# The last block of a fused recurrence and MLP kernel: two single-quadrant products in banks of their own, and the fallback path as a loop

## The chip, the cores and the metric

One core of a Trainium2 chip. The time is device microseconds of one execution, 2330.94 us for the kernel before (median of three runs, 2330.39 to 2331.64). Besides it this document uses a second measure: the **tail**, read from a trace. Its zero, the **anchor**, is the start of a product of one column, called `most`, 2.1 us before the end of the last product of the last block. Tail times are written +3.86 and so on. **END** is the span's end counted from the anchor.

In the views, PE is TensorE, DVE VectorE, ACT ScalarE and POOL GpSimd; SPq and ACTq are the instruction queues of SyncE and ScalarE, and L542 is line 542 of the kernel's file. An instruction page is a piece of the program that a DMA brings to an engine, in these traces 16 KB for TensorE and 8 KB for the others (in the kernel before 85 packets with 1.39 MB and 63 with 0.52 MB); the page of a kernel is the printed profile. Each of the last two stores by SyncE lands in 16 parts, each with its own event in the trace.

## The reference, cut to what matters

```python
f = lower_bound + (1.0 - lower_bound) * sigmoid(f_logit)   # (4, 6080, 256)
for t in range(S):
    h = f[:, t] * h + (1.0 - f[:, t]) * x[:, t]
    y[:, t] = h
h = y.reshape(24320, 256) @ w_in      # 256 -> 2048
g = h - tanh(h)
out = g @ w_out                       # 2048 -> 256, float32
```

## The kernel before

The 24320 tokens are 48 blocks (one of 256, then 512 each). Both matrix products use a scheme with seven products of quadrants in place of eight; a polynomial stands for h - tanh(h) where h is small. Squares of h are watched, and if any was too large, a path for large h (`general`) computes everything again. With these inputs it never runs: at the end every engine reads a flag and jumps over it.

The second matrix product runs over four units per block, each adding into four tiles Qa, Qb, Qc, Qd of PSUM, the memory that TensorE writes its products to. Two products go into one half of Qd each, and so to a single quadrant of the result:

```python
PARTS = (
    (("Qa", 0, A11, "h", 0), ("Qa", 1, S1, "T", 0)),
    (("Qb", 0, A12, "h", 3), ("Qb", 1, S2, "h", 1)),
    (("Qc", 0, S3, "T", 1),),
    (("Qd", 0, S4, "h", 2), ("Qd", 1, A22, "T", 2)),
)

def second_layer(n, part):
    j, u = units[n]
    products = PARTS[part]
    ...
    for c in range(2):
        for _, r, slot, right, q in products:      # alternates between the halves
            nc.tensor.matmul(acc[j, part][:, r, 0 : st[n]["hb"]], ...)
```

For the last block the result is transposed by TensorE and stored in two halves:

```python
def end(j):
    ...
    for half in range(2):
        slot, r = ((2, 1), (1, 0))[half]
        nc.vector.tensor_tensor(
            out=C[:, slot], in0=acc[j, 3][:, r, 0:hb], in1=C[:, slot], op=ALU.add
        )
        name = ("Qa", "Qb")[half]
        bank = ps_b.tile([P, 2, KC, P], FP32, name=name, tag=name)
        for i in range(2):
            for k in range(KC):
                nc.tensor.transpose(
                    bank[:, i, k], C[:, 2 * k + half, i * P : (i + 1) * P], ident[:]
                )
        rows = osb[:, 2 * half : 2 * half + 2]
        (nc.scalar.copy, nc.vector.tensor_copy)[half](
            out=rows.rearrange("p i (m k) -> p i k m", k=KC), in_=bank[:]
        )
        t0 = starts[j] + half * hb
        nc.sync.dma_start(
            out=out[t0 : t0 + hb, :].rearrange("(i p) d -> p i d", p=P), in_=rows
        )
```

And the program's last lines:

```python
    fast()
    seen = nc.values_load(flag[:].bitcast(INT32), ...)
    with tc.If(seen != 0):
        general()          # 48 blocks, unrolled
```

## Time and profile before

| before | |
|---|---|
| time | 2330.94 us |
| TensorE, share of the chain that ended last | 99% |
| last product ends | anchor + 2.13 us |
| output stores issued by SyncE | +3.86, +4.44 |
| TensorE branches, goes on | +3.67, 3.91 us later |
| last part of the last store lands | +8.32 |
| END | +9.39 |

The prediction shows the page's first lines and the chain. The profile's page counts instruction packets of the whole run (columns: packets, MB, share of 16 engines' span); q8 is read as TensorE's queue, q14 as that of the other engines:

```profile
q8 instruction: 85, 1.39, 0.3%
q14 instruction: 63, 0.52, 0.1%
```

### The profile page before, as it was taken

The numbers are of one execution on the slowest core, as the hardware profiler recorded it, in microseconds if no ns is written. First come the engines' busy times: TensorE is split into PE (matmuls) and PEld (weight loads), VectorE is DVE, ScalarE is ACT, GpSimd is POOL, SyncE is SP. The second block draws the span as 40 slices with busy tenths as digits, with TensorE's granted clock in tenths as the row PEclk, the third lists the DMA queues.
The fourth block names the chain that finished last, engine by engine and source line by source line (L and its number), as shares of the span: only waits on it lengthen the run. The fifth ranks groups of instructions, "written<-read, shape, count | busy, mean of one in ns | idle before, by whom it ended". The sixth has DMA issues, their size and how long they took to land.

```text
span 2330.1 us, 28649 instructions
## 1 busy us (share of the span) xinstructions
PE 2318.8 (100%) x10676; PEld 2025.3 (87%) x10676; DVE 2121.3 (91%) x2447; ACT 1800.6 (77%) x2686; POOL 0.7 (0%) x6
## 2 busy tenths in 40 slices
PE   9999999999999999999999999999999999999998
PEld 5888888888888888888888888888888888888887
DVE  8999899998999989999899999999899998999987
ACT  7777777777777777787777777777777777777775
POOL 0000000000000000000000000000000000000000
PEclk9999999999999999999999999999999999999999
DMA  6311211112111111111111121111211112111101
GB/s 172 64 23 29 45 37 28 28 33 41 37 28 28 37 37 37 28 28 40 33 37 28 28 44 30 37 28 28 46 28 37 28 28 46 31 33 28 28 10 29
DMA packets 296948, 85.05 MB, mean 36 GB/s; under 512 B 289888, under 2 KB 292704, under 8 KB 296800
## 3 DMA queue, kind: packets, MB, share of 16 engines
q1 hardware_dynamic: 296512, 82.87, 16.9%
q8 instruction: 85, 1.39, 0.3%
q14 instruction: 63, 0.52, 0.1%
q10 hardware_dynamic: 288, 0.26, 0.0%
HBM read 58.20 MB, written 24.90 MB: 36 GB/s over the span
## 4 chain that ended last, share of the span: by engine, by line
PE 99%; DMA 0%; DVE 0%; issue 0%; ACT 0%; SPq 0%
PE A L388 27%; PE Qd L471 14%; PE Qa L471 14%; PE D L388 14%; PE Qb L471 14%; PE B L388 7%; PE Qc L471 7%; PE A L687 1%; PE Qc L754 1%; PE Qa L754 1%; PE Qb L754 1%; PE D L687 0%; PE Qd L687 0%; PE B L687 0%; DMA fn<-in_f_logit_dram 0%; PE Qa L687 0%
## 5 line engine op out<-in xcount | busy, mean ns | idle before, releaser
L388 PE MATMUL A<-T,w_in 128*128 128x256 f32 x2208 | 558.8, 379 | 0.0
L388 PEld LDWEIGHTS A<-T,w_in 128*128 128x128 f32 x2208 | 419.5, 190 | 57.0
L432 DVE TENSOR_TENSOR h<-h,q 128x1024 f32<-128x1024 f32 x368 | 437.6, 1220 | 3.1
L426 DVE SCALAR_TENSOR_TENSOR q<-q,t 128x1024 f32<-128x1024 f32 x368 | 440.0, 1216 | 0.0
L419 ACT ACTIVATE q<-t 128x1024 f32<-128x1024 f32 x368 | 382.8, 1053 | 46.7 <-DVE h L432 43.8
L416 ACT ACTIVATE t<-h 128x1024 f32<-128x1024 f32 x368 | 388.6, 1056 | 3.1 <-DVE h L403 0.3
L437 ACT ACTIVATE junk<-t 128x1024 bf16<-128x1024 f32 x368 | 388.1, 1055 | 1.5
L451 DVE TENSOR_TENSOR Tg<-h 128x1024 f32<-128x1024 f32 x368 | 348.0, 946 | 6.4
L471 PE MATMUL Qb<-h,w_out 128*128 128x256 f32 x1472 | 347.7, 379 | 0.0
L471 PEld LDWEIGHTS Qb<-h,w_out 128*128 128x128 f32 x1472 | 279.7, 190 | 38.0
L471 PE MATMUL Qd<-h,w_out 128*128 128x256 f32 x736 | 219.0, 379 | 0.0
L471 PE MATMUL Qa<-Tg,w_out 128*128 128x256 f32 x736 | 219.0, 379 | 0.0
L471 PE MATMUL Qa<-h,w_out 128*128 128x256 f32 x736 | 218.9, 379 | 0.0
L471 PE MATMUL Qd<-Tg,w_out 128*128 128x256 f32 x736 | 218.9, 379 | 0.0
L400 ACT COPY h<-B 128x512 f32<-128x512 f32 x184 | 106.9, 581 | 143.0 <-PE B L388 94.2
L400 ACT COPY h<-A 128x512 f32<-128x512 f32 x184 | 107.2, 583 | 136.7 <-PE A L388 125.3
L403 DVE TENSOR_TENSOR h<-D,r 128x512 f32<-128x512 f32 x184 | 126.9, 689 | 92.7 <-PE D L388 89.1
L403 DVE TENSOR_TENSOR h<-A,r 128x512 f32<-128x512 f32 x184 | 126.3, 687 | 73.8 <-PE A L388 42.1
L400 ACT COPY r<-A 128x512 f32<-128x512 f32 x184 | 107.2, 583 | 105.9 <-PE A L388 105.9
L388 PE MATMUL D<-T,w_in 128*128 128x256 f32 x736 | 188.9, 379 | 0.0
L388 PE MATMUL A<-y,w_in 128*128 128x256 f32 x736 | 188.9, 379 | 0.0
L388 PE MATMUL B<-y,w_in 128*128 128x256 f32 x736 | 188.9, 379 | 0.0
(120 smaller groups left out, 3069.2 us busy)
## 6 DMA issues: line engine op xcount, KB each, us to landing
xn<-in_x_dram SPq DMA_DIRECT2D x184, 128.0 KB, 3.3
fn<-in_f_logit_dram SPq DMA_DIRECT2D x184, 128.0 KB, 3.1
out_dram<-osb SPq DMA_DIRECT2D x180, 128.0 KB, 2.8
raw<-in_moe_w_out_dram SPq DMA_DIRECT2D x8, 512.0 KB, 4.9
raw<-in_moe_w_in_dram SPq DMA_DIRECT2D x7, 512.0 KB, 4.7
out_dram<-osb SPq DMA_DIRECT2D x3, 256.0 KB, 3.9
fn<-in_f_logit_dram SPq DMA_DIRECT2D x1, 512.0 KB, 7.3
xn<-in_x_dram SPq DMA_DIRECT2D x1, 512.0 KB, 8.2
```

The source lines that it names most:

```text
L388: nc.tensor.matmul(ps[:, c], lhsT=w_in[u][:, slot, c * P : (c + 1) * P], rhs=mixes[j][right], start=start and c == 0, stop=True, skip_grou ...
L400: nc.scalar.copy(out=dst, in_=piece(n, bank))
L403: nc.vector.tensor_tensor(out=piece(n, "h")[:, q], in0=piece(n, bank), in1=piece(n, r), op=ALU.add)
L416: nc.scalar.activation(out=half(n, i, "t"), in_=half(n, i), func=AF.Square)
L419: nc.scalar.activation(out=half(n, i, "q"), in_=half(n, i, "t"), func=AF.Square, scale=RA, bias=RB,)
L426: nc.vector.scalar_tensor_tensor(out=q, in0=q, scalar=RC, in1=t, op0=ALU.add, op1=ALU.mult)
L432: nc.vector.tensor_tensor(out=h, in0=h, in1=q, op=ALU.mult)
L437: nc.scalar.activation(out=junk[:, :, :, 0 : st[n]["hb"]], in_=t, func=AF.Relu, bias=-TINY, accum_out=flags[:, 2 * n + i : 2 * n + i + 1],)
L451: nc.vector.tensor_tensor(out=o, in0=a, in1=b, op=ALU.subtract)
L471: nc.tensor.matmul(acc[j, part][:, r, 0 : st[n]["hb"]], lhsT=w_out[u][:, slot, c * P : (c + 1) * P], rhs=piece(n, right)[:, q, c], start=( ...
L687: nc.tensor.matmul(h[c], lhsT=w_in[u][:, 2 * k + s, c * P : (c + 1) * P], rhs=ys[j][:, k, 0:nb], start=k == 0 and (c == 0 or len(banks) == 2),
L754: nc.tensor.matmul(acc[j][i // 2][:, i % 2].rearrange("p (k m) -> p k m", k=2), lhsT=plain[j, u][:, s, c, i * P : (i + 1) * P], rhs=w_out[ ...
```

## The change

Its intent: let the first of the last two quadrants be complete four passes earlier, shorten the relay of additions, transposes and copies behind the last product, and shrink the code that is jumped over. Three parts, cut to the core:

```diff
+            alone = [ps_a.tile([P, TB], FP32, name="A", tag="A")[:, 0:hb] for _ in range(2)]
+            for half, (slot, right, q) in enumerate(((A22, "T", 2), (S4, "h", 2))):
+                for c in range(2):
+                    nc.tensor.matmul(alone[half], lhsT=w_out[NU - 1][:, slot, ...],
+                                     rhs=piece(n, right)[:, q, c], start=c == 0, stop=c == 1)
             for half in range(2):
-                slot, r = ((2, 1), (1, 0))[half]
+                slot = 2 - half
                 nc.vector.tensor_tensor(
-                    out=C[:, slot], in0=acc[j, 3][:, r, 0:hb], in1=C[:, slot], op=ALU.add
-                )
-                name = ("Qa", "Qb")[half]
-                bank = ps_b.tile([P, 2, KC, P], FP32, name=name, tag=name)
+                    out=C[:, slot], in0=alone[half], in1=C[:, slot], op=ALU.add
+                )
+            for half in range(2):
                 for i in range(2):
-                    for k in range(KC):
+                    name = ("Qa", "Qb", "Qc", "D")[2 * half + i]
+                    bank = ps_b.tile([P, KC, P], FP32, name=name, tag=name)
+                    for k in (0, 1) if half == 0 else (1, 0):
                         nc.tensor.transpose(...)
-                (nc.scalar.copy, nc.vector.tensor_copy)[half](
-                    out=rows.rearrange("p i (m k) -> p i k m", k=KC), in_=bank[:]
-                )
+                    (nc.scalar.copy, nc.vector.tensor_copy)[i](
+                        out=osb[:, 2 * half + i].rearrange("p (m k) -> p k m", k=KC),
+                        in_=bank[:],
+                    )
                 nc.sync.dma_start(...)
...
+                    if final and (name, u) == ("Qd", NU - 2):
+                        kept = mixpool.tile([P, 4, HB], FP32, name="T")
+                        acc[j, "kept"] = kept
+                        nc.scalar.copy(out=kept[:, 0:2], in_=acc[j, 3][:, :, 0 : sizes[j] // 2])
...
     def general(ctx):
-            for j, nb in enumerate(sizes):              # 48 blocks, unrolled
+        with tc.For_i(0, S, H) as t0:                   # 190 steps of 4 x 32 tokens
+            with tc.manual_schedule():
```

The sums of the first three units are copied out of Qd (`kept`) and added early by `part_end` (not shown), which also splits the addition of 512 columns into three of 256.

More of the change, by code (lines that the diff above doesn't have):

```diff
@@ L78 @@
     srcs = [a.rearrange("b s d -> (b s) d") for a in (f_logit, x)]
+    ALL = len(sizes)
+    sizes.append(B * H)
+    assert B * H <= P and S % H == 0
     const = ctx.enter_context(tc.tile_pool(name="const", bufs=1))
@@ L521, in give, with part_end @@
                 )
+        def part_end(j, step):
+            hb = sizes[j] // 2
+            p, kept = acc[j, "p"][:, :, 0:hb], acc[j, "kept"]
+            if step == "o1":
+                finish(j, 1)
+            if step == "p15":
+                nc.vector.tensor_tensor(
+                    out=kept[:, 2], in0=p[:, 1], in1=kept[:, 0], op=ALU.add
+                )
+                return
+            C = acc[j, "C"][:, 0 : 4 * hb].rearrange("p (n t) -> p n t", n=4)
+            for o, a, b in {
+                "o1": (),
+                "o2": ((kept[:, 3], acc[j, 2][:, 0, 0:hb], C[:, 1]),),
+                "o3": (
+                    (C[:, 2], kept[:, 3], kept[:, 1]),
+                    (C[:, 1], C[:, 1], kept[:, 2]),
+                    (C[:, 3], kept[:, 3], p[:, 1]),
+                ),
+            }[step]:
+                nc.vector.tensor_tensor(out=o, in0=a, in1=b, op=ALU.add)
@@ L523, in end @@
         def end(j):
-            hb = sizes[j] // 2
+            hb, n = sizes[j] // 2, j * NU + NU - 1
             C = acc[j, "C"][:, 0 : 4 * hb].rearrange("p (n t) -> p n t", n=4)
             osb = opool.tile([P, NQ, D], FP32, name="osb", tag="osb")
+            alone = [ps_a.tile([P, TB], FP32, name="A", tag="A")[:, 0:hb] for _ in range(2)]
+            for half, (slot, right, q) in enumerate(((A22, "T", 2), (S4, "h", 2))):
+                for c in range(2):
+                    nc.tensor.matmul(
+                        alone[half],
+                        lhsT=w_out[NU - 1][:, slot, c * P : (c + 1) * P],
+                        rhs=piece(n, right)[:, q, c],
+                        start=c == 0,
+                        stop=c == 1,
+                    )
@@ L536, in end @@
                 for i in range(2):
-                    for k in range(KC):
+                    name = ("Qa", "Qb", "Qc", "D")[2 * half + i]
+                    bank = ps_b.tile([P, KC, P], FP32, name=name, tag=name)
+                    for k in (0, 1) if half == 0 else (1, 0):
                         nc.tensor.transpose(
-                            bank[:, i, k], C[:, 2 * k + half, i * P : (i + 1) * P], ident[:]
+                            bank[:, k], C[:, 2 * k + half, i * P : (i + 1) * P], ident[:]
@@ L540, in end @@
                         )
-                rows = osb[:, 2 * half : 2 * half + 2]
-                (nc.scalar.copy, nc.vector.tensor_copy)[half](
-                    out=rows.rearrange("p i (m k) -> p i k m", k=KC), in_=bank[:]
-                )
+                    (nc.scalar.copy, nc.vector.tensor_copy)[i](
+                        out=osb[:, 2 * half + i].rearrange("p (m k) -> p k m", k=KC),
+                        in_=bank[:],
+                    )
                 t0 = starts[j] + half * hb
@@ L546, in end @@
                 nc.sync.dma_start(
-                    out=out[t0 : t0 + hb, :].rearrange("(i p) d -> p i d", p=P), in_=rows
+                    out=out[t0 : t0 + hb, :].rearrange("(i p) d -> p i d", p=P),
+                    in_=osb[:, 2 * half : 2 * half + 2],
                 )
@@ L903, in fast @@
                         continue
+                    final = j == NBLK - 1
+                    if final and (name, u) == ("Qd", NU - 1):
+                        continue
                     if u is None:
-                        if (name, j) == ("o1", NBLK - 1):
+                        if final and name == "o1":
                             nc.vector.reduce_max(
@@ L908, in fast @@
                             )
-                        if j == NBLK - 1 and name in ("o4", "otr"):
-                            if name == "o4":
-                                end(j)
+                        if final and name == "o3":
+                            sum_up()
+                        if final and name == "o4":
+                            end(j)
+                        if final and name[0] == "o":
+                            if name in ("o1", "o2", "o3"):
+                                part_end(j, name)
                             continue
-                        if (name, j) == ("o3", NBLK - 1):
-                            sum_up()
                         steps[name](j)
@@ L917, in fast @@
                             fetch(j + 1)
+                        if final and name == "p15":
+                            part_end(j, name)
                         continue
                     steps[name](j * NU + u)
+                    if final and (name, u) == ("Qd", NU - 2):
+                        kept = mixpool.tile([P, 4, HB], FP32, name="T")
+                        acc[j, "kept"] = kept
+                        nc.scalar.copy(
+                            out=kept[:, 0:2], in_=acc[j, 3][:, :, 0 : sizes[j] // 2]
+                        )
     @with_exitstack
     def general(ctx):
-        fetch, steps, ys = recurrence(ctx)[0:3]
+        _, steps, ys, natpool, _, nats, chan = recurrence(ctx)
         wpool = ctx.enter_context(tc.tile_pool(name="w", bufs=1))
@@ L933, in general @@
         w_out = [wpool.tile([P, 2, 2, D], FP32, name=f"w_out{u}") for u in range(NU)]
+        y = wpool.tile([P, KC, B, H], FP32, name="y")
+        carry = wpool.tile([P, KC, B], FP32, name="carry")
+        nb = B * H
         def temp(tag, dtype=FP32):
@@ L938, in general @@
         with tc.manual_schedule():
+            nc.vector.memset(carry[:], 0.0)
             for u in range(NU):
@@ L950, in general @@
                         rounding[step]()
-            for j, nb in enumerate(sizes):
-                ns = nb // P
-                fetch(j, queue=nc.gpsimd)
-                for step in ("tf", "tx", "sg", "f0", "f1", "v0", "v1", "sc0", "sc1"):
-                    steps[step](j)
-                ps = ps_o.tile([P, NQ, D], FP32, name="psO")
+        with tc.For_i(0, S, H) as t0:
+            with tc.manual_schedule():
+                for s, src in enumerate((f_logit, x)):
+                    nat = natpool.tile([P, TB // H, KC * H], FP32, name=("fn", "xn")[s])
+                    part = src[:, bass.ds(t0, H), :].rearrange("j b (i c) -> i b j c", i=G)
+                    for i in range(G):
+                        nc.gpsimd.dma_start(out=nat[i * H : (i + 1) * H, 0:B, :], in_=part[i])
+                    nats[ALL, s] = nat
+                for step in ("tf", "tx", "sg", "f0", "f1", "v0", "v1"):
+                    steps[step](ALL)
+                for k in range(KC):
+                    for b in range(B):
+                        nc.vector.tensor_tensor_scan(
+                            out=y[:, k, b], data0=chan[ALL, "f", k][:, b * H : (b + 1) * H],
+                            data1=chan[ALL, "v", k][:, b * H : (b + 1) * H],
+                            initial=carry[:, k, b : b + 1], op0=ALU.mult, op1=ALU.add,
+                        )
+                nc.vector.tensor_copy(out=carry[:], in_=y[:, :, :, H - 1])
+                ps = ps_o.tile([P, D], FP32, name="psO")[0:nb]
                 for u in range(NU):
                     for s in range(2):
-                        hT = ps_h.tile([P, 2, TB], FP32, name="hT")
+                        hT = ps_h.tile([P, 2, HB], FP32, name="hT")
                         for c in range(2):
@@ L964, in general @@
                                     lhsT=w_in[u][:, k, s, c * P : (c + 1) * P],
-                                    rhs=ys[j][:, k, 0:nb],
-                                    start=(k == 0),
+                                    rhs=y[:, k].rearrange("p j b -> p (j b)"),
+                                    start=(c == 0 and k == 0),
                                     stop=(k == KC - 1),
+                                    skip_group_check=True,
                                 )
@@ L973, in general @@
                         ]
-                        gT = gpool.tile([P, 2, TB], FP32, name="gT")
+                        gT = gpool.tile([P, 2, HB], FP32, name="gT")
                         g = gT[:, :, 0:nb]
@@ L992, in general @@
                         for c in range(2):
-                            for i in range(ns):
-                                nc.tensor.matmul(
-                                    ps[:, i, :],
-                                    lhsT=gT[:, c, i * P : (i + 1) * P],
-                                    rhs=w_out[u][:, s, c, :],
-                                    start=(u == s == c == 0 and i % 2 == 0),
-                                    stop=(u == NU - 1 and s == c == 1),
-                                    skip_group_check=True,
-                                )
-                osb = opool.tile([P, NQ, D], FP32, name="osb")
-                nc.scalar.copy(out=osb[:, 0:ns, :], in_=ps[:, 0:ns, :])
-                nc.gpsimd.dma_start(
-                    out=out[starts[j] : starts[j] + nb, :].rearrange(
-                        "(i p) d -> p i d", p=P
-                    ),
-                    in_=osb[:, 0:ns, :],
-                )
+                            nc.tensor.matmul(
+                                ps,
+                                lhsT=gT[:, c, 0:nb],
+                                rhs=w_out[u][:, s, c, :],
+                                start=(u == s == c == 0),
+                                stop=(u == NU - 1 and s == c == 1),
+                            )
+                osb = opool.tile([P, D], FP32, name="osb")
+                nc.scalar.copy(out=osb[0:nb], in_=ps)
+                dst = out.rearrange("(j t) d -> j t d", j=B)[:, bass.ds(t0, H), :]
+                for b in range(B):
+                    nc.gpsimd.dma_start(out=dst[b], in_=osb[b * H : (b + 1) * H])
     fast()
```

## The prediction

The two lines of figures among the first marks are times read in the trace of the kernel before: from a branch to the engine's next instruction, then of VectorE's additions. The 0.4, a quarter of 1.5, is the author's estimate. "Less than one page" is an estimate too: in the trace of before one page comes every 27.6 us (between 24 and 30 in the main loop), and a product with its weight load, two instructions, takes 0.216 us, so a page has about 256 instructions, against the 192 that are jumped over. That so short a jump brings no page, the point against rival (a), was not shown. The granted clock was 0.999.

> **What bounds the kernel now.** I read the whole-kernel page first (busy shares, then the chain that ended last), then the groups by line, then, because the change touches only the last of 48 blocks of tokens, the chain, the timeline and the DMA view of the last 30 us.
>
> ```profile
> span 2330.1 us, 28649 instructions
> PE 2318.8 (100%) x10676; PEld 2025.3 (87%) x10676; DVE 2121.3 (91%) x2447; ACT 1800.6 (77%) x2686; POOL 0.7 (0%) x6
> PE 99%; DMA 0%; DVE 0%; issue 0%; ACT 0%; SPq 0%
> ```
>
> TensorE is the bound: 99% of the chain that ended last, at a full granted clock. Its 10676 matmul records start about 0.216 us apart and leave no gap. The change takes no matmul away and adds none: the listing of both instruction streams has 5363 matmul instructions ahead of the final branch in each, in the same order up to the last block's last unit. So some 2320 us of the 2330 cannot move. What can move is the tail, after the last product that TensorE owes. The chain of waits there:
>
> ```profile
> 2319.93 0.86 PE Qc L471 x4
> 2320.79 0.12 PE most L845 x2
> 2320.91 1.94 PE Qd L471 x8
> 2322.85 0.02 issue
> 2322.87 0.44 DVE C L531
> 2323.31 0.04 issue
> 2323.35 0.55 PE Qa L538 x3
> 2323.90 0.51 PE Qb L538 x4
> 2324.41 0.02 issue
> 2324.44 0.69 DVE osb L542
> ```
>
> From 2322.85 on this is a serial relay: last product, an addition (DVE), four transposes (PE), four more, a copy (DVE), then the second output store. In the trace that store is issued at 2325.16 and its last part lands at 2329.04; the closing waits and barriers take from there to the end of the span at 2330.11, 1.07 us. So 7.3 us follow the last product, 3.9 of them the last store. Why the store takes so long is seen in the DMA view of the microsecond in which its packets start:
>
> ```profile
> DMA  0000009000000000990143596988979698968998
> q8 instruction: 1, 0.02, 8.5%
> q14 instruction: 2, 0.02, 7.2%
> out_dram<-osb SPq DMA_DIRECT2D x1, 256.0 KB, 3.9
> ```
>
> Besides the store, three instruction pages are being fetched. These follow the skipped branch: every engine jumps over the unrolled path for large h. In the trace TensorE reaches its compare-and-branch at 2324.39; a 16 KB instruction packet runs on one DMA engine from 2325.44 for 1.36 us; TensorE goes on at 2328.29. ScalarE branches at 2324.48 and goes on at 2327.12, VectorE 2325.07 and 2328.31. Twelve of the 16 parts of the second store have landed by 2327.47 (2.31 us after issue); the other four land at 2327.69, 2327.84, 2328.27 and 2329.04. In the microsecond from 2327 nearly one DMA engine alone is moving 1 KB packets, one each 42 ns: I read it as the engine that carried the 16 KB page first and then worked off its 32 packets of the two stores.
>
> [...]
> [...] 2.6 to 3.9 us from branch to next instruction, with a page fetch about 0.7 to 1.4 us after each branch (pages of 16 KB on TensorE's queue, 8 KB on the others). SyncE, with almost nothing to jump over, goes on after 0.19 us.
> [...] 691 ns for 512 columns, 416 to 425 for 256. Back to back, though, the two 256-column additions start 0.34 us apart.
> [...]
>
> **The change, part by part.**
>
> *Products.* Today the last eight passes into Qd alternate between the two halves, both complete at 2322.85. Now the four passes of A22 x T go first into a bank of their own and the four of S4 x h after them. The first set is done four passes, 4 x 0.216 = 0.86 us, sooner: 2321.99. The second still ends at 2322.85. PE time is unchanged.
>
> *Additions.* What Qd held from the first three units is copied out (ACT, 128x512, 0.58 us, at about 2314.7 where ACT stands idle for 5.2 us: free), plus one DVE addition at 2318.9 (0.42, before Qb is done at 2319.94: free; the maximum of the flags moves about 0.4 us but is wanted only at 2320.7). The addition of 512 columns (0.69) becomes three of 256: starts 2321.29, 2321.63, 2321.97, DVE free at about 2322.31. The first final addition then runs 2322.31 to 2322.73 (DVE sets it, not the product), the second waits for its product as before: 2322.87 to 2323.30. Both precede every copy.
>
> *Transposes.* Today two phases of four: half 0 waits until 2323.35, half 1 until 2323.74, last end 2324.40. Now half 0 needs 2322.73, so its transposes run at about 2322.78 to 2323.27, and the ready quadrant of half 1 follows at once. Only three are left after the last addition (2323.35, then 0.11 apart): last start 2323.57, end 2323.85.
>
> *Copies.* Two of 512 (0.62 ACT, 0.69 DVE) become four of 256 (about 0.40 ACT from the 256-column output copies of the first blocks, 0.42 DVE), each half shared by both engines. Half 0: both done at about 2323.74, store issued 2323.76 instead of 2324.58. Half 1: DVE from 2323.88 to 2324.30, store at 2324.33 instead of 2325.16. Gain: **0.83 us**. SyncE needs about 0.58 us from one store to the next, and has it.
>
> *Loop.* Never executed: the flag is zero here. But the skipped code shrinks: TensorE had 4576 matmul instructions to jump over and has 48, some 192 machine instructions, or less than one page; VectorE and ScalarE have roughly 100 to 150 instead of over 1700 rows. [...] If no page lay in the stores' way, the last part would land 2.4 us after issue as the others do, not 3.9: up to **1.5 us** more. I count about a quarter of it. TensorE's 16 KB page came about when the next sequential page was due anyway (one every 27.6 us; the one before at 2295.83), so a fetch may fall on the stores whatever the branch does; and since the branch comes earlier too, so does its fetch.
>
> Sum: 0.83 + 0.4 = about 1.3 us off 2330.94, or 2329.6.
>
> **Rivals.**
> (a) *The fetch stays and hides the rest.* The end is set by the DMA engine with the 16 KB page. TensorE's branch moves only from 2324.39 to about 2323.95, so page and packets behind it end just 0.4 us sooner; the earlier copies then win nothing. For it: the page due anyway. Against: 192 instructions fit in one page. Time 2330.5.
> (b) *No fetch at all.* The full 0.83 + 1.5: 2328.6. For it: SyncE's short jump at 0.19 us. [...]
> (c) *VectorE becomes the bound.* If the three additions start 0.42 instead of 0.34 apart, DVE is free at 2322.55, the first addition ends 2322.97 and the second slips by 0.1. Loss 0.1 to 0.2 us: 2329.8.
> (d) *The loop's bookkeeping is paid on the skipped side*: more semaphores to set right, 0.06 us each in SyncE's closing waits; mostly they pass before the store lands. At most 0.3 us.
>
> **Range and chances.** The three runs before spread over 1.25 us, as much as the expected gain. From (b) with some luck to (a) with noise: 2328.2 to 2330.8. A gain of 2% would need 46 us and only the last 8 us are touched; the same holds for a loss, unless the schedule of the main loop changed, and the streams say it did not. Within 2%: 0.99; faster 0.005; slower 0.005.
>
> **What would show each step right or wrong.** Chain: the last 256-column copy on DVE should end at 2324.3, with both final additions done by 2323.3; a later first addition speaks for (c). Stores issued at about 2323.8 and 2324.3. DMA view of the last 6 us: if TensorE's queue still shows its 16 KB page and one engine's tail runs on, (a); if instruction packets of the whole run fall from 85 and 63 by several and the last landing comes 2.4 us after issue, (b). Wrong altogether if block spacing in the middle of the kernel changes, or if any engine resumes from its branch later than the last landing.

## More of the kernel before

SyncE's waits, for the first of the two stores (us in total, times, longest): one wait, on the copy. The wait is part of the store's own instruction, which starts 0.017 us after the copy's signal (+3.845).

```profile
SPq L546 <- ACT osb L542: 4.0, 1, 4.0
```

The DMA view of 5 us from anchor + 3.40 (40 slices of 0.125 us; in the last line: size of a store, us from issue to the landing of its last part):

```profile
GB/s 0 0 0 0 0 0 0 0 66 0 197 205 319 270 262 319 344 320 418 320 287 328 311 115 66 57 49 49 49 33 25 90 25 25 25 16 0 0 66 131
q8 instruction: 2, 0.03, 3.3%
q14 instruction: 5, 0.04, 3.0%
out_dram<-osb SPq DMA_DIRECT2D x2, 256.0 KB, 3.9
```

Some 300 GB/s for a microsecond and a half, and then 1.6 us of mostly 16 to 66: that low shelf, not the bulk, sets the landing. The 66 and the 131 at the right end are instruction pages again (8 KB and 16 KB).

## The result, and the profile after

Six runs of each: 2331.03 us (2330.05 to 2331.74), before 2331.81 (2330.39 to 2332.45). Ratios here are the mean time of one kernel's fast runs over that of the other's of the same rounds, so not quite the ratio of the medians quoted: 0.9997, 95% interval 0.9984 to 1.001, which is -3.7 to +2.3 us. The time lies 0.23 us above the predicted range.

The page of the kernel after, its first lines and the chain's shares:

```profile
span 2328.9 us, 28658 instructions
...
PE 2318.8 (100%) x10674; PEld 2024.9 (87%) x10676; DVE 2121.6 (91%) x2451; ACT 1802.2 (77%) x2688; POOL 0.7 (0%) x6
...
q8 instruction: 84, 1.38, 0.3%
q14 instruction: 59, 0.48, 0.1%
...
PE 99%; DMA 0%; SPq 0%; issue 0%; DVE 0%
```

The bound is the same. The instruction packets fell by one and by four only, although thousands of skipped instructions are gone. The chain of the last microseconds (start, duration, engine, what):

```profile
2319.78 0.12 PE most L886 x2
2319.90 1.93 PE A L561 x8
2321.82 0.26 PE Qa L578 x2
2322.09 0.22 PE Qb L578 x2
2322.30 0.36 PE Qc L578 x2
2322.67 0.23 PE D L578 x2
...
2322.92 0.42 DVE osb L581
```

In the kernel before, `most` stood at 2320.79 in the same view (where it is counted from the end of the product before it; its record starts at 2320.72), so 1.01 has to be subtracted from the times of the prediction before they are compared. The transposes are then where the step *Transposes* put them, and the relay has lost its two DVE additions: they hide behind TensorE. The timeline of the same stretch (start, duration, engine, instruction; in brackets the idle time before it and what ended that):

```profile
2321.29 0.41 DVE L570 TENSOR_TENSOR C<-A,C 128x256 f32<-128x256 f32 x1
2321.86 0.42 DVE L570 TENSOR_TENSOR C<-A,C 128x256 f32<-128x256 f32 x1 [0.16 <-PE A L561]
...
2322.34 0.42 DVE L581 COPY osb<-Qb 128x256 f32<-128x256 f32 x1
...
2322.92 0.42 DVE L581 COPY osb<-D 128x256 f32<-128x256 f32 x1 [0.16 <-PE D L578]
2323.13 0.91 SPq L586 DMA_DIRECT2D out_dram<-osb  x2
```

First addition at 2321.29 (predicted 2322.31 - 1.01 = 2321.30), second at 2321.86 (2321.86), last copy at 2322.92 (2322.87). But half 0 lies copied at 2322.76, and SyncE issues its store at 2323.13. SyncE's waits show what is new there:

```profile
SPq L586 <- DVE osb L581: 3.3, 1, 3.3
```

Half 0 now needs two engines' copies. In the trace SyncE's stream has a separate wait instruction for DVE's copy ahead of the store; it ends at 2322.80, and the store starts 0.33 us later. The stores are issued at +3.42 and +3.93 in place of +3.86 and +4.44: 0.51 us earlier at the second, not 0.83.

And then the 0.51 us is lost. The DMA view of the same 5 us from the anchor:

```profile
GB/s 0 0 0 0 0 66 0 246 287 311 270 344 352 328 393 320 279 319 336 197 49 33 33 33 41 25 25 25 16 25 25 25 25 25 8 0 0 0 0 0
q8 instruction: 1, 0.02, 2.1%
q14 instruction: 2, 0.02, 1.2%
out_dram<-osb SPq DMA_DIRECT2D x2, 256.0 KB, 4.1
```

The bulk is some 0.4 us sooner, but the low shelf is longer and ends at about the same slice. The last part lands 4.20 us after issue (before: 3.88), at +8.13 (before: +8.32). TensorE's 16 KB instruction page is still there: it runs from +4.34 to +5.99 (before: +4.72 to +6.07).

### The profile page after: what moved, and what is told of

The parts are those of the page before. It is cut to its first block, busy times and chain, and to the rows that moved or that the text cites. A ratio compares the mean times of both kernels' runs of the same rounds, so it can differ in the third digit from the quotient of the medians.

```text
span 2328.9 us, 28658 instructions
## 1 busy us (share of the span) xinstructions
PE 2318.8 (100%) x10674; PEld 2024.9 (87%) x10676; DVE 2121.6 (91%) x2451; ACT 1802.2 (77%) x2688; POOL 0.7 (0%) x6
## 4 chain that ended last, share of the span: by engine, by line
PE 99%; DMA 0%; SPq 0%; issue 0%; DVE 0%
PE A L392 27%; PE Qa L475 14%; PE D L392 14%; PE Qb L475 14%; PE Qd L475 14%; PE B L392 7%; PE Qc L475 7%; PE Qa L795 1%; PE Qc L795 1%; PE Qb L795 1%; PE A L728 1%; PE D L728 0%; PE Qd L728 0%; DMA xn<-in_x_dram 0%; PE B L728 0%; PE A L561 0%
```

## The experiments

Sixteen runs, three of them repeats of the two kernels. All gave correct results; the three without the branch are right only for inputs without large h. Eight ran on one chip (b1, a1, l1, e1, n1, p1, np1, d1), four on a second (f1, d2, f2, a2), three on a third (nb1, g1, f4) and f5 on a fourth. A profile was taken of each, and the table gives its tail; "page" is TensorE's 16 KB packet near the branch. Single runs of the first eight stood beside one run before at 2332.01, those of the second and third chip beside 2330.72 and 2330.52 (medians of nine). For a2, f2, f4 and f5 the time is the median of five timed runs, for the others a single run. A single run's state is unknown; the timed ones used are all fast, and no granted clock was under 0.998.

| kernel | run, us | stores issued | TensorE branches, goes on after | page | last landing | END |
|---|---|---|---|---|---|---|
| before | | 3.86, 4.44 | 3.67, 3.91 | 4.72-6.07 | 8.32 | 9.39 |
| b1 (before again) | 2329.72 | 3.86, 4.44 | 3.67, 3.71 | 4.71-5.91 | 8.11 | 9.18 |
| after | | 3.42, 3.93 | 3.23, 0.43 | 4.34-5.99 | 8.13 | 9.20 |
| a1 (after again) | 2330.71 | 3.43, 3.93 | 3.23, 0.42 | 4.31-5.90 | 8.05 | 9.11 |
| a2 (after, timed) | 2331.02 | 3.43, 3.94 | 3.22, 0.42 | 4.31-5.88 | 8.02 | 9.09 |
| l1 (loop alone) | 2331.91 | 3.86, 4.44 | 3.66, 0.42 | 4.75-6.27 | 8.41 | 9.48 |
| e1 (end alone) | 2332.11 | 3.43, 3.94 | 3.22, 4.39 | 4.25-6.04 | 8.36 | 9.43 |
| n1 (after, no branch) | 2327.97 | 3.43, 3.93 | none | none | 6.40 | 7.36 |
| nb1 (before, no branch) | 2328.2 | 3.86, 4.44 | none | none | 6.79 | 7.74 |
| p1 (pages shifted) | 2332.0 | 3.43, 3.94 | 3.22, 0.42 | 4.31-5.85 | 7.96 | 9.03 |
| np1 (shifted, no branch) | 2329.95 | 3.43, 3.93 | none | -5.59 to -4.67 | 6.35 | 7.30 |
| d1 | 2330.07 | 3.43, 3.94 | 3.23, 0.43 | 4.32-5.60 | 7.64 | 8.71 |
| d2 | 2331.36 | 3.27, 3.78 | 3.23, 0.49 | 4.30-5.64 | 7.68 | 8.75 |
| g1 | 2331.34 | 3.11, 3.78 | 3.23, 0.43 | 4.89-5.83 | 7.53 | 8.59 |
| f1 | 2330.91 | 3.43, 3.94 | 5.24, 0.43 | 6.62-7.55 | 7.28 | 8.35 |
| f2 | 2330.58 | 3.27, 3.78 | 5.26, 0.42 | 6.34-7.27 | 7.14 | 8.20 |
| f4 | 2330.35 | 3.27, 3.78 | 5.84, 0.42 | 6.94-8.27 | 7.09 | 8.15 |
| f5 | 2329.06 | 3.27, 3.78 | 5.86, 0.42 | 6.95-7.94 | 6.33 | 7.40 |

### How much is noise: both kernels again

Edit: none.

> The kernel before, unchanged, for a second profile. The tail is measured from the start of the one-column product (most) on TensorE, because the opening alone moves every later event by about 1 us between two runs. In the first profile: second store issued at +4.44 us, its last part landed at +8.32, end of the span at +9.39. If the tail is a fixed sequence, these come back within 0.1 us; if the DMA part is random, the landing moves by several tenths.

> The changed kernel, unchanged, for a second profile. First profile: first store at +3.42, second store issued at +3.93 after the start of most, last part landed at +8.13, end of the span at +9.21. Fixed sequence: the same within 0.1 us. In particular the first store started 0.33 us after its VectorE wait was over and just after the second ScalarE copy: if that is a true wait it comes back; if chance, the store starts at +3.12.

> The changed kernel, timed beside the others of this call. The tails say 0.1 to 0.3 us less than the kernel before, far below the run-to-run spread of about 0.7 us that the opening makes; ratio 0.9995 to 1.0.

The work between the first product into Qa of the whole run and the anchor took 2301.89 or 2301.90 us in every kernel but two (p1 2301.96, np1 2303.43, the latter unexplained). The anchor itself lies anywhere from 2318.68 to 2321.68 us, within one kernel too (before: 2320.72, b1: 2318.74): the opening, ahead of the first products, differs by up to 3 us from run to run. That is more than anything in the tail, and it is why the tail is compared from the anchor. By the traces END is 9.39 and 9.18 before, mean 9.29, and 9.20, 9.11, 9.09 after, mean 9.13: **0.15 us** less, no more than two profiles of one kernel differ by (0.21 us for before, where the landing, not the issue of the stores, moved). The profiles come from several chips; a1 and a2, on two of them, have the same store times to 0.01 us and END to 0.02. Five timed runs of a2 over nine of before: 1.0001, interval 0.9988 to 1.0015.

### The two halves of the change alone

l1 is the kernel before with the new `general`; e1 the kernel after with the old one.

```diff
 # l1: end(), the additions and Qd as before;   e1: the reverse
-            for j, nb in enumerate(sizes):
+        with tc.For_i(0, S, H) as t0:
```

> The loop alone, with the old end. Theory A (the 16 KB page that delays the last store is TensorE's next page in order, due there anyway): TensorE goes on from its branch within 0.5 us instead of 3.9, yet a 16 KB page still runs at about +4.7 to +6.1 and the last part lands at +8.3, end at +9.4, as before. Rival B (the page is the branch's target, and the shorter jump takes it away): no 16 KB page after the branch, last landing 2.4 us after the second store, at +6.9, end at +8.0.

> The new end alone, with the old unrolled path for large h. Theory A: second store issued at +3.93 as in the changed kernel, TensorE stalls 3.9 us at its branch but is back before the last landing, page at +4.3, last landing about +8.1, end +9.2: the loop is worth nothing. Rival B: with far jumps more pages are fetched in the way of the stores than in the changed kernel, and the end comes at +9.4 or later.

Neither gains by itself: END 9.48 and 9.43. l1 came out as Theory A said, e1 at the figure of Rival B; but the 0.2 us between the two readings of e1 are no more than two profiles of one kernel differ by. The loop does what was hoped for TensorE, which goes on 0.42 us after the branch in place of 3.7 to 4.4. But its page stays. The DMA view of l1, 5 us from anchor + 3.40:

```profile
GB/s 0 0 0 0 0 0 0 0 0 0 156 254 336 319 287 344 344 369 311 303 319 295 311 99 16 16 25 41 49 41 25 16 25 25 25 25 16 0 0 0
q8 instruction: 1, 0.02, 1.9%
...
out_dram<-osb SPq DMA_DIRECT2D x2, 256.0 KB, 4.0
```

The same shelf as before, with one page on each queue in place of two and five. Which of the two holds the last part back, l1 cannot tell; f1 and f5 below separate them.

### Without the branch

```diff
     fast()
-    seen = nc.values_load(...)
-    with tc.If(seen != 0):
-        general()
```

> The changed kernel without the branch and without the path for large h (right for these inputs only). Times from the start of most. If TensorE's 16 KB page at +4.3 is the next page in order, due by count before the branch, it is still there and the last part lands near +8.1, end +9.1. If it is fetched because the jump, some 240 instructions long, lands in the next page, it is gone: last landing 2.4 us after the second store, +6.4, and the end at about +7.4.

> The kernel before without its branch and path for large h (right for these inputs only). Stores at +3.86 and +4.44 as in the kernel before. If the page fetched at the branch is all that hides the new end's gain, the last part lands 2.4 us after the second store, at +6.86, and the end is at +7.85: 0.5 us after the changed kernel without branch (+7.36), where with the branch the two differ by 0.0 to 0.3. If the end of the two is the same without the branch too, something else levels them.

The DMA view of n1, the same 5 us:

```profile
GB/s 0 0 0 0 0 66 0 115 319 344 311 369 352 344 352 344 352 344 352 254 33 8 0 0 0 0 0 0 0 0 0 0 0 0 0 0 0 0 0 0
q14 instruction: 1, 0.01, 0.6%
...
out_dram<-osb SPq DMA_DIRECT2D x2, 256.0 KB, 2.3
```

No packet on q8, and no shelf: every part of both stores lands within 2.47 us of issue (in after the last one took 4.20). END falls by 1.8 us for the kernel after (9.13 to 7.36) and 1.5 for the kernel before (9.29 to 7.74). Part of END's fall is shorter closing work (0.96 from the last landing to the end, 1.07 with a branch). Between the two kernels without the branch the change is worth 7.74 - 7.36 = **0.38 us** (0.44 with np1 below, 7.30): so the new end does gain, where nothing hides it. (n1 and nb1 ran on different chips, one profile each.)

### Is the page due by count, or is it the jump's?

The prediction held that TensorE's page was due at that point by the count of instructions. p1 puts 102 more instructions into TensorE's stream early on, which by an estimate shifts every page boundary by 11 us (102 at half of 0.216 us):

```diff
-            for _ in range(n):
+            for _ in range(4 * n):
                 nc.tensor.matmul(
-                    busy[:], lhsT=zeros.bitcast(BF16)[:, 0:P],
-                    rhs=zeros.bitcast(BF16)[:, 0:TB], ...
+                    busy[:, 0:P], lhsT=zeros.bitcast(BF16)[:, 0:P],
+                    rhs=zeros.bitcast(BF16)[:, 0:P], ...
```

> The changed kernel with each dummy product of the opening split into four of 128 columns: 102 more TensorE instructions for the same time, so every page boundary comes 102 instructions, about 11 us, sooner at the end of the kernel. Page due by count: 16 KB page at about -7, none at the branch unless the jump itself crosses a boundary; then last landing +6.4, end +7.4. Page due to the jump: a page at +4.3 again and the end at +9.1 (the jump of 240 starts 102 into a page and crosses one).

> Both: no branch and the shifted pages. No 16 KB page after about -7 in either reading. If that page is what holds up one DMA engine, the last part of the second store lands 2.4 us after its issue like the others (+6.4), and the end is at about +7.4, 1.7 us sooner than the changed kernel. If one part of a store lands late whatever is fetched, the landing stays about 4 us after issue and the end near +9.

In p1 the page due by count comes at -5.73, and a second one at +4.31, 1.09 us after the branch, as in the kernel after (1.11 after it). In np1, shifted and without a branch, only the early one is there. So the page near the branch belongs to the jump. In n1 no page fell due in the tail at all.

### The 0.33 us in front of the first store

d1 swaps the engines of half 1's two copies, d2 those of half 0, g1 gives half 0 to ScalarE alone and half 1 to VectorE alone.

```diff
-                    (nc.scalar.copy, nc.vector.tensor_copy)[i](
+                    (nc.scalar.copy, nc.vector.tensor_copy)[i ^ half](          # d1
+                    (nc.scalar.copy, nc.vector.tensor_copy)[i ^ (half == 0)](   # d2
+                    (nc.scalar.copy, nc.vector.tensor_copy)[half](              # g1
```

> The changed kernel with the two engines of the second half's copies swapped (ScalarE copies the later bank). The first store starts at +3.42 although what it waits for is done at +3.10, and 0.03 us after the second half's ScalarE copy. If it somehow waits for that copy, it now starts at about +3.64 and the second store at +4.15. If the 0.33 us are something else (SyncE itself), the stores stay at +3.42 and about +3.93.

> The changed kernel with the engines of the first half's copies swapped (VectorE the first bank, ScalarE the second), so that the ScalarE copy, which the store instruction waits for itself, ends last, at about +3.02, rather than the VectorE copy, which a separate wait instruction of SyncE waits for. If the 0.33 us before the first store belong to that separate wait, the first store starts at +3.05 and the second at +3.67. If not, they stay at +3.43 and +3.93. The end stays with the page, near +8.9, either way.

> The changed kernel with the first half copied by ScalarE alone and the second by VectorE alone, as before, so that neither store has a copy in SyncE's separate wait instruction. If the 0.33 us come after a long separate wait, the first store starts 0.02 us after the second ScalarE copy, at about +3.2, and the second at about +3.85. If the 0.33 us belong to any store of the changed end, the first starts at +3.5. The end stays with the page, +8.7 to +9.2.

d1: ScalarE's second copy now ends at +3.61, and store 0 still begins at +3.43: it does not wait for that copy by mistake. d2: DVE's copy for half 0 comes first, its separate wait ends at +2.94, and the store begins at +3.27, again 0.33 later: neither of the two times that were expected (+3.05 and +3.43). g1: half 0 needs one engine only, the wait sits in the store instruction itself, and the store begins at +3.11, 0.017 us after the signal of ScalarE's second copy, as in the kernel before. (The view of SyncE's waits names ScalarE's branch there, with 3.6 us: a later signal of the same semaphore. The copy's own stands at +3.095 in the trace.)

So 0.33 us goes with a separate, long wait instruction of SyncE ahead of a store. Why it takes that long stays open: at 39.5 us another separate long wait (9.1 us, in after) was followed by its DMA, a load, after 0.04 us. Note what the earlier stores bring: in g1 they are issued up to 0.31 us before those of after, with a last landing at 7.53, 7.64 in d1 with stores not a bit earlier. The landing follows the end of the page. From page end to last landing it is 2.25 us (before), 2.20 (b1), 2.14 (after), 2.15, 2.14, 2.14 (l1), 2.32 (e1), 2.11 (p1), 2.04 (d1), 2.04 (d2), whether the last store was issued at 3.78 or at 4.44; 1.70 in g1, where the page came late.

### Holding the branches back

If the jump's page is what delays the stores' last parts, an engine that jumps later, when the stores' packets have gone, should free them, without the branch or the path for large h being given up. f1 makes TensorE wait at the very end for a result of ScalarE that nobody needs; f2 adds d2's copies, which f4 and f5 keep; f4 delays TensorE a little more; f5 delays VectorE's jump as well.

```diff
                 nc.sync.dma_start(...)
+            late = tpool.tile([P, 4, HB], FP32, name="late", tag="t")
+            nc.scalar.activation(out=late[:], in_=acc[j, "kept"][:], func=AF.Square)
+            nc.scalar.activation(out=late[:, 0:2], in_=late[:, 0:2], func=AF.Square)   # f4, f5
+            nc.vector.tensor_copy(out=worst[:], in_=late[:, 3, 0:1])                   # f5
+            after = ps_b.tile([P, TB], FP32, name="B", tag="B")
+            nc.tensor.matmul(
+                after[0:1, 0:1], lhsT=late[:, 0, 0:1], rhs=ones[:], start=True, stop=True
+            )
```

> The changed kernel, the branch and loop kept, with TensorE's branch held back: after the last copies ScalarE does one more operation on 1024 columns (1.06 us, result unused), and a 1x1 product on TensorE waits for it. TensorE then branches near +5.1 instead of +3.2 and its page starts near +6.1, when the stores have been moved. If the page at the branch is what delays the last landing: last landing +6.4, end +7.4. If it comes at another time or something else holds the store: end stays near +9.

> Late branch and swapped copies together. With both reasons right: stores at +3.05 and +3.67, last landing +6.1, end +7.1, that is 2.1 us less than the changed kernel and 2.3 less than before; a ratio of 0.999 to the kernel before, at the edge of what five rounds resolve.

> As f2, with one more ScalarE operation of 512 columns (0.58 us) ahead of TensorE's branch: it branches near +5.85, goes on at +6.27, and its page starts at +6.9 or later, when the last part of the store (+6.2) is down. End +7.2 to +7.4, so 1.8 us less than the changed kernel. If the page still catches the last part, the end stays near +8.2. Ratio to the kernel before 0.999, perhaps not resolved.

> As f4, with VectorE's branch held back too, by a one-column copy that waits for the first late ScalarE operation: it branches near +5.0 instead of +3.84, so its 8 KB page comes near +6.5 instead of +5.74. If that page is what leaves one part of the second store at 3.3 us after issue in f1, f2 and f4, all parts land within 2.5 us of the issue, the last at about +6.2, and the end is at +7.3. If the part is late for another reason, the end stays near +8.2.

f1 moves TensorE's page to +6.62 and the last landing to +7.28; END falls by 0.78 against the mean of after, to 8.35 where 7.4 was expected; f2 and f4 miss their expectations in the same way (8.20 and 8.15). One part of store 1 still took 3.34 us, and in f4, with TensorE's page later still (+6.94), one part still took 3.30. VectorE jumps at +3.84 in both, and an 8 KB page follows it (+5.74 to +6.04 in f4). f5 moves that jump to +5.24; its page then runs from +6.39, after the last landing. (ScalarE does the extra operations, so its own branch is later too, +5.16 in place of +3.54; that was so in f4 already and changed nothing there.) The timeline of f5 at that place, then its DMA view of 5 us from anchor + 3.40:

```profile
2325.07 0.15 DVE L593 COPY worst<-late 128x1 f32<-128x1 f32 x1 [0.72 <-ACT late L591]
2325.75 0.19 PE L595 MATMUL B<-ones,late 128*1 128x1 f32 x2 [1.86 <-ACT late L592]
```

```profile
GB/s 0 0 0 0 66 0 147 328 319 303 385 369 344 344 328 360 352 336 230 33 16 0 0 66 0 0 0 0 131 0 0 0 0 0 0 0 0 0 0 0
q14 instruction: 2, 0.02, 1.4%
q8 instruction: 1, 0.02, 1.2%
out_dram<-osb SPq DMA_DIRECT2D x2, 256.0 KB, 2.4
```

The 66 and the 131 are now behind the bulk, and the shelf is gone. All parts land within 2.55 us, and END is **7.40**: 1.73 less than the mean of after, 1.88 less than the mean of before, with the branch and the path for large h in place; 0.15 us of it can be d2's earlier stores. Timed in five rounds: 2329.06 us (2328.13 to 2330.27) against 2331.35 of before (nine runs, 2330.55 to 2332.26), ratio 0.9991, interval 0.9977 to 1.0004. That has the size the tail gives (1.88 us would be 0.9992), but the interval includes 1: timed runs alone do not establish it. f2 and f4 lie at 0.9998 (0.9984 to 1.0012) and 0.9997 (0.9983 to 1.001).

## Why the prediction was right or wrong, point by point

- TensorE's 2301.9 us in the middle are the same in both kernels to 0.01 us.
- **The range** failed first at its base. It was built on three runs with a median of 2330.94; with three more, all six have 2331.81. The opening moves a run's total by up to 3 us, and a range of 2.6 us, cut from three runs and the argument's own rivals, was too narrow for it. Of the 1.43 us between 2329.6 and 2331.03, the base is 0.87.
- **Products, Additions, Transposes, Copies** were right to about 0.05 us in every time up to the last copy, rival (c) did not happen (the additions start 0.34 apart), and rival (d) is not seen: from the last landing to the end it is 1.07 us in both.
- **"Store issued 2323.76 ... Gain: 0.83 us"** was mis-sized: 0.51. The predicted times are +3.04 and +3.61 from the anchor; the stores stand at +3.42 and +3.93. The step overlooked that the first store, which needs two engines' copies, gets a separate wait instruction on SyncE (after and d2; in before and g1, where one engine copies all of half 0, the wait is the store's own); with it came 0.33 us at the first store, and the second follows 0.51 behind the first. ("SyncE needs about 0.58 us" was misread: in the kernel before the second store waited for VectorE's copy, whose signal came at +4.42, 0.02 us before it.)
- **Loop, "I count about a quarter of it"**: 0.4 us expected, none found with the old end (l1: END 9.48, before 9.18 and 9.39); with the new end one profile shows 0.3 (e1: 9.43, after 9.09 to 9.20), little more than the scatter. The estimate rested in part on a passage by which most of the short jumps would need no page; no trace had shown that. With the loop every engine does go on soon, 0.18 to 0.59 us after its branch (after: ScalarE 0.18, SyncE 0.19, TensorE 0.43, GpSimd 0.47, VectorE 0.59), where with the unrolled path all but SyncE (0.19) took 2.6 to 3.9 us (before; TensorE 4.39 in e1). But the short jump brings a 16 KB packet too (l1: +4.75, before: +4.72), and stores that meet it land as late as with the long jump (l1: +8.41, before: +8.32 and +8.11). Why a short jump fetches anything is not shown. Rival (b) falls with it.
- **The sum** is the step that failed most: it added the two gains, about 1.3 us, as if both reached the end, where END shows 0.15. **Rival (a) happened**: the end hangs on TensorE's page, which moved 0.4 us earlier with its branch (4.72 to 4.34). By the mean END 0.15 us of that is seen; the page packets themselves take between 0.9 and 1.8 us from run to run, which is more. Rival (a)'s 2330.5 was an effect of -0.44 on its base, nearer to the -0.78 between the medians than the -1.3 predicted; but -0.78 is itself within the noise. The reason I gave for it, a page due by count, was wrong, so that it came true is in part luck: n1 and np1 have no page there, p1 has both.
- **The spread of the store's landings** was read rightly in kind: take the jumps out (n1, nb1) or hold them back (f5) and the last part of a store lands within 2.2 to 2.6 us. That it is one DMA engine that works through the page and then through its share of the stores is inferred from the 25 GB/s of the shelf, where in after the 1 KB packets start 42 ns apart (by an estimate 21.5 GB/s for each of 16 engines in n1's bulk of some 344); the trace doesn't name the engine. "Nearly one DMA engine alone" was too much for the microsecond from 2327: the store's packets there fill 19.6% of 16 engines, some three, and 1.7 in its second half.
- **The shared bank** is not what made the first addition late: in the old order the last pass of all belongs to A22 x T, the product that the first addition needs. The new order makes it early: in after it starts at 2321.29, while TensorE writes the other bank until 2321.83. Whether it needs a bank of its own for this is not shown: no run put the new order into one bank.

What stays open: the cause of the 0.33 us, why a short jump brings a page, and the spread of the opening.

## What to carry to other kernels

Before you shorten a relay that ends in a store, look at what else the DMA view shows beside that store: here instruction pages fetched for engines that had already finished (TensorE's from +4.34 to +5.99) took back most of what the relay won (0.51 us at the second store, 0.15 at END). Holding the branches of TensorE and VectorE back by 2.6 and 1.4 us brought END down by 1.7 us in one profile, where the whole change brought 0.15. That an engine goes on quickly after its branch (0.42 us in l1) didn't make the branch free here (its page at +4.75, END 9.48); look for the page in the DMA view. Where runs differ by more than the effect, measure from a fixed instruction near the end in several traces, and take a range for the total from the spread of many runs, not of three.
